# Three more warm-up matmuls of zeros in the prologue of an attention-plus-MLP kernel

## The chip, the core and the metric

The kernel runs on one core of one Trainium2 chip. The metric is the device time of one execution in microseconds (us); the median of several runs is compared. The profile is of one such execution and names the engines PE (TensorE's matmuls), PEld (TensorE's weight loads, which overlap the matmuls), DVE (VectorE), ACT (ScalarE), POOL (GpSimd) and SP (SyncE, which only issues transfers here).

## The reference

There are 8 batches and 8 heads, with 512 tokens and 32 state rows of 64 features in each. Tokens read the state and the state reads the tokens, both through a softmax; the results, 4352 rows of 512, then go through a two-layer MLP with SiLU.

```python
# x: (8, 8, 512, 64)   state: (8, 8, 32, 64)
a      = softmax(x @ state.T / 8)        # over the 32 state rows
xread  = a @ state
a2     = softmax(state @ x.T / 8)        # over the 512 tokens
sread  = a2 @ x
rows   = concat([xread, sread], axis=2)  # heads side by side: (4352, 512)
h      = rows @ w_in                     # (512, 2048)
g      = h * sigmoid(h)
out    = g @ w_out                       # (2048, 512), float32
```

## The kernel before

The schedule is written by hand: each engine executes its instructions in the order in which the program states them, and semaphores order the engines among one another. Matmuls take bf16 operands and sum in float32.

For each batch the first MLP layer is merged with the state: `w1_cols` (L336) multiplies the transposed state `stT` by `w_in` and evicts the product as `W1`. The attention weights are computed per group of four heads (`hg` 0 and 1): `scores` (L230), `exps` (L242, on ACT), `norm` (L252 to L255: sums and reciprocals on DVE, the product `an` on POOL or DVE) and a transpose into `aT`, which for batch 0 TensorE does itself (`pe_transpose_a`, L272). `emit_G1` (L362) multiplies W1 by aT and applies SiLU on ACT; `G2` (L391) multiplies the result by `w_out`, summing over 16 chunks of features, and `store` evicts and writes the rows. The state's own reads go through `token_sums`, `sread` (L293, L303) and a last pass at the end (L372, L413). From batch 0 on, the loops over `tt` and `ft` weave the next batch's attention in between the matmuls of the present one.

The change lies in the prologue. What it touches, in program order:

- SP issues the state of batch 0 (`st0_f`, the profile's `st_f`) and x of batch 0 in two halves of four heads (`x_f`, L139). POOL builds the identity and issues the first loads of `w_in`, `w_out` and the whole state (`st_b`).
- DVE clears `busy`, a tile of zeros, and `stT`.
- `keep_busy(n, pool, tag)` (L129) has TensorE multiply zeros by zeros n times, 128x128 by 128x512, into a PSUM tile of the given pool that nobody reads. Nothing waits for these matmuls except what is behind them in TensorE's own order, and later users of that PSUM buffer.
- The first `keep_busy` stands ahead of the transposes of batch 0's state (L163). DVE then copies these in four pieces into `stT` (L123).
- The second `keep_busy` follows, ahead of the transposes of x (L186), which wait for DVE's cast of x to bf16 (`cast_x`, L100, tile `x_nat`).
- After both groups' scores and exponentials, `w1_cols` for 256 columns and five loads issued by POOL, the third `keep_busy` stands ahead of the transposes of `an` (L272).

Of the kernel before, what the change touches and what calls it, by code (L numbers as in the profile page):

```python
# [36 lines left out]
def kernel(  # L37
# [20 lines left out]
    psO = ctx.enter_context(tc.tile_pool(name="psO", bufs=2, space=bass.MemoryType.PSUM))  # L58
    psH = ctx.enter_context(tc.tile_pool(name="psH", bufs=2, space=bass.MemoryType.PSUM))
# [34 lines left out]
    def load_x(b):  # L94
        nc.gpsimd.dma_start(x_f[:], x[b].rearrange("h (p c) d -> p h c d", p=128, c=4))  # L95
# [23 lines left out]
    def copy(eng, dst, src):  # L119
        if eng is nc.scalar:  # L120
            nc.scalar.activation(dst, src, func=COPY, bias=0.0)  # L121
        else:
            eng.tensor_copy(dst, src)  # L123


    def keep_busy(n, pool, tag):
        ps = pool.tile([128, 512], FP32, tag=tag, name="ps_busy")
        for _ in range(n):
            nc.tensor.matmul(  # L129
                ps[:], busy[:, 0:128], busy[:], start=True, stop=True, skip_group_check=True  # L130
            )
# [24 lines left out]
    )  # L156


    keep_busy(6, psH, "h1")
    copy(nc.vector, st0_n[:], st0_f[:])  # L160
    ps0 = bank([128, 4, NS], BF16, "ps_st0")
    for kt in range(4):
# [3 lines left out]
    for g in range(2):  # L166
        for u in range(2):
# [2 lines left out]
                stT[ds(64 * u, 64), 0, ds(2 * g, 2), u ^ g, :],  # L170
                ps0[ds(64 * u, 64), ds(2 * g, 2), :],
            )
    keep_busy(3, psH, "h1")

# [92 lines left out]
    def pe_transpose_a(b, hg, eng):  # L269
        ps = bank([128, 4, 128], BF16, "ps_at")  # L270
        for c in range(4):
            nc.tensor.transpose(ps[:, c, :], an[b, hg][:, c, :, :], ident[:])  # L272
        copy(eng, aT[b][:, hg, :, :], ps[:])
# [79 lines left out]
    h1 = {}  # L353
# [91 lines left out]
    load_w_in(1536)  # L445
    load_w_out(12, 4)
    load_x(1)
    keep_busy(3, psO, "o")
    pe_transpose_a(0, 0, nc.vector)
    pe_transpose_a(0, 1, nc.vector)  # L450

# [148 lines left out]
```

## Time and profile before

| | us |
|---|---|
| median of 5 runs | 225.04 |
| lowest and highest | 224.52 and 227.21 |
| the profiled execution's own time | 224.52 |
| its span, first to last instruction | 222.5 |
| PE busy | 211.4 (95%) |
| PEld busy | 100.8 (45%) |
| DVE busy | 104.9 (47%) |
| ACT busy | 142.4 (64%) |
| POOL busy | 45.7 (21%) |

A line of a timeline gives the start, the time from there to the end of the last of its instructions, the engine, the line of the kernel, what is written and read, and how many instructions are merged in it; in square brackets stands how long the engine had been idle before and what ended that. A line of the chain of waits has start, length and what it was; the chain runs backwards from the last instruction through whatever released each step. In the table by stretch, the columns are the stretch, its length, then busy time and count of PE, PEld, DVE, ACT and POOL, the granted TensorE clock as a share of full speed, the DMA share, and GB/s. The ends of matmuls are modelled: their starts are the surer record.

### The profile page before, as it was taken

The page shows a single profiled execution, that of the slowest core. Times are in us where ns is not written, and L with a number is a line of the kernel's source. Part 1 is how long each engine was busy: PE and PEld are TensorE (multiplying, and loading weights), DVE is VectorE, ACT ScalarE, POOL GpSimd, SP SyncE. Part 2 cuts the span into 40 slices and gives each one's busy share as a digit, 9 for nine tenths or more (in the row PEclk, how much of TensorE's full clock was granted, in tenths as well). Part 3 has the DMA queues.
Part 4 walks back from the last instruction along what each step waited for, and adds up shares of the span by engine and source line. Part 5 has one row for each costly group of instructions (what it writes and reads, how often), then busy time and mean ns, then how long its engine had stood idle before and what let it go on. Part 6 is the DMA issues. An engine that isn't in the chain of part 4 may idle for free.

```text
span 222.5 us, 3716 instructions
## 1 busy us (share of the span) xinstructions
PE 211.4 (95%) x1462; PEld 100.8 (45%) x1488; DVE 104.9 (47%) x183; ACT 142.4 (64%) x241; POOL 45.7 (21%) x64
## 2 busy tenths in 40 slices
PE   7689899999989999999999999999999999999993
PEld 2434235445425443545344444454454445466652
DVE  5665856452975075525644382629260836010011
ACT  2655469899555985588577947695759675834410
POOL 8480001800800045002700090008000300000000
PEclk9999999999999999999999999999999999999998
DMA  5999955393375115911594138504700330111112
GB/s 190 198 205 205 213 183 199 134 246 104 98 238 122 47 48 133 292 48 47 102 253 120 50 94 248 134 0 110 177 16 32 86 107 0 47 47 50 47 47 94
DMA packets 32209, 26.78 MB, mean 120 GB/s; under 512 B 20160, under 2 KB 26048, under 8 KB 32192
## 3 DMA queue, kind: packets, MB, share of 16 engines
q1 hardware_dynamic: 25376, 14.75, 24.2%
q0 software_dynamic: 6816, 11.80, 23.4%
q8 instruction: 11, 0.18, 0.3%
q14 instruction: 6, 0.05, 0.1%
HBM read 17.37 MB, written 8.91 MB: 118 GB/s over the span
## 4 chain that ended last, share of the span: by engine, by line
PE 84%; DVE 10%; issue 2%; ACT 1%; POOL 0%; DVEq 0%; POOLq 0%
PE o L391 44%; PE h L362 24%; PE ps_w L336 4%; PE h L372 3%; PE ps_sc L230 2%; DVE es_f L282 2%; DVE stT L123 2%; PE o_half L413 2%; DVE rb L312 2%; PE ps_sr L303 1%; DVE W L123 1%; PE ps_busy L129 1%; DVE xmT L316 1%; DVE rs L252 1%; ACT exp_nat L242 1%
## 5 line engine op out<-in xcount | busy, mean ns | idle before, releaser
L391 PE MATMUL o<-w_out_sb,g 128*128 128x512 bf16 x488 | 132.6, 379 | 1.0 <-issue 0.2
L383 ACT ACTIVATE g<-h 128x512 bf16<-128x512 f32 (+1 forms) x144 | 82.0, 573 | 41.5 <-PE h L362 27.2
L362 PE MATMUL h<-aT,W 128*128 128x512 bf16 x256 | 75.5, 379 | 2.3 <-DVE W L123 1.5
L391 PEld LDWEIGHTS <-g 128*128 128x128 bf16 x528 | 49.7, 98 | 58.1 <-issue 6.4
L123 DVE COPY o_sb<-o 128x512 f32<-128x512 f32 x17 | 11.8, 692 | 62.8 <-PE o L391 62.7
L362 PEld LDWEIGHTS <-W 128*128 128x128 bf16 x256 | 24.6, 98 | 32.3 <-DVE W L123 3.7
L255 POOL TENSOR_TENSOR an<-exp_nat,rc 128x512 bf16<-128x512 bf16 (+1 forms) x16 | 15.9, 1009 | 109.9 <-DVE rc L253 109.7
L123 DVE CAST W<-ps_w 128x512 bf16<-128x512 f32 (+1 forms) x31 | 20.0, 676 | 18.7 <-PE ps_w L336 18.7
L121 ACT ACTIVATE W<-ps_w 128x512 bf16<-128x512 f32 (+1 forms) x35 | 18.7, 575 | 11.4 <-PE ps_w L336 11.3
L312 DVE RECIPROCAL rb<-ps_sr 128x256 f32<-128x256 f32 x8 | 14.0, 1750 | 16.2 <-PE ps_sr L303 16.2
L121 ACT ACTIVATE o_sb<-o 128x512 f32<-128x512 f32 x15 | 8.9, 597 | 14.3 <-PE o L391 6.1
L282 DVE TENSOR_REDUCE es_f<-exp_nat 128x128 f32<-128x512 bf16 x16 | 15.5, 1013 | 0.2
L100 POOL CAST x_nat<-x_f 128x512 bf16<-128x512 f32 x24 | 14.7, 646 | 0.0
L336 PE MATMUL ps_w<-w_in_sb,stT 64*32 64x512 bf16 (+1 forms) x264 | 11.6, 376 | 0.6 <-DVE stT L123 0.4
L252 DVE TENSOR_REDUCE rs<-exp_nat 128x16 f32<-128x512 bf16 x16 | 10.6, 660 | 1.9 <-ACT exp_nat L242 1.2
L95 POOL DMA_DIRECT2D x_f<-in_x_dram x7 | 6.5, 926 | 19.8 <-DVE x_nat L100 18.3
L316 DVE TENSOR_TENSOR xmT<-ps_sr,rb 64x64 bf16<-64x64 f32 x32 | 9.6, 299 | 0.6
L372 PE MATMUL h<-xmT,w_in_sb 128*128 128x256 bf16 x64 | 9.6, 273 | 0.0
L242 ACT ACTIVATE exp_nat<-ps_sc 128x512 bf16<-128x512 f32 x16 | 8.8, 595 | 0.9 <-PE ps_sc L230 0.8
L372 PEld LDWEIGHTS <-w_in_sb 128*128 128x128 bf16 x64 | 6.3, 98 | 3.9
L242 ACT ACT_TABLE_LOAD x6 | 7.7, 1283 | 0.2 <-PE ps_sc L230 0.2
L537 ACT ACT_TABLE_LOAD x6 | 7.7, 1283 | 0.1
(56 smaller groups left out, 100.7 us busy)
## 6 DMA issues: line engine op xcount, KB each, us to landing
out_dram<-o_sb SPq DMA_DIRECT2D x33, 256.0 KB, 2.3
x_f<-in_x_dram POOLq DMA_DIRECT2D x7, 1024.0 KB, 7.1
w_in_sb<-in_moe_w_in_dram POOLq DMA_DIRECT2D x3, 512.0 KB, 10.1
w_out_sb<-in_moe_w_out_dram POOLq DMA_DIRECT2D x3, 512.0 KB, 12.0
x_f<-in_x_dram SPq DMA_DIRECT2D x2, 512.0 KB, 4.3
w_in_sb<-in_moe_w_in_dram POOLq DMA_DIRECT2D x2, 256.0 KB, 7.2
w_out_sb<-in_moe_w_out_dram POOLq DMA_DIRECT2D x2, 256.0 KB, 7.7
st_b<-in_state_dram POOLq DMA_DIRECT2D x1, 256.0 KB, 12.3
```

The source lines that it names most:

```text
L100: eng.tensor_copy(x_nat[b][:, ds(c0, nc_), ds(h0, nh), :], x_f[:, ds(h0, nh), ds(c0, nc_), :].rearrange("p h c d -> p c h d"),)
L121: nc.scalar.activation(dst, src, func=COPY, bias=0.0)
L123: eng.tensor_copy(dst, src)
L242: nc.scalar.activation(e[:], sc_ps[hg][:], func=EXP, bias=0.0, scale=SCALE)
L255: eng.tensor_tensor(a[:, ds(c, n)], e[:, ds(c, n)], rc[:, ds(c, n)].to_broadcast([128, n, 4, NS]), op=MULT,)
L282: nc.vector.tensor_reduce(f[:, hg], exp_nat[b, hg].rearrange("p c s n -> p s n c"), axis=AX, op=ADD)
L312: nc.vector.reciprocal(rb[:], ps[:, 1, :, :, :])
L336: nc.tensor.matmul(pss[f, hg][ds(32 * s, 32), 0:n], stT[ds(r, 64), b, h // 2, s % 2, :], w_in_sb[ds(r, 64), h // 2, ds(f, n)], start=True, ...
L362: nc.tensor.matmul(ps[:], W1[b][:, hg, ds(128 * ft, 128)], aT[b][:, hg, :, :], start=(hg == 0), stop=(hg == 1), skip_group_check=True,)
L372: nc.tensor.matmul(ps[:, 0:256], w_in_sb[:, kt, ds(128 * ft, 128)], xmT[:, :, kt].rearrange("p t n b -> p t (n b)"), start=(kt == 0), stop ...
L383: nc.scalar.activation(g[:, 0:n], ps[:, 0:n], func=SILU, bias=0.0)
L391: nc.tensor.matmul(outs[tt][:], gt[b * NFT + ft][:, ds(128 * tt, 128)], w_out_sb[:, ft, :], start=(ft == 0), stop=(ft == NFT - 1), skip_gr ...
```

## The change

Each of the three calls of `keep_busy` gets one more matmul of zeros: 6 becomes 7, and 3 becomes 4 twice. Everything else is as it was.

```diff
-    keep_busy(6, psH, "h1")
+    keep_busy(7, psH, "h1")
     copy(nc.vector, st0_n[:], st0_f[:])
     ps0 = bank([128, 4, NS], BF16, "ps_st0")
     for kt in range(4):
...
-    keep_busy(3, psH, "h1")
+    keep_busy(4, psH, "h1")
...
     load_w_out(12, 4)
     load_x(1)
-    keep_busy(3, psO, "o")
+    keep_busy(4, psO, "o")
     pe_transpose_a(0, 0, nc.vector)
     pe_transpose_a(0, 1, nc.vector)
```

## The prediction, made before the result was known

> **What bounds the kernel now.** I read the page first, then the chain of waits in order of time, then the timeline of the first 14 us, where the edit lies.
>
> ```profile
> span 222.5 us, 3716 instructions
> ...
> PE 211.4 (95%) x1462; PEld 100.8 (45%) x1488; DVE 104.9 (47%) x183; ACT 142.4 (64%) x241; POOL 45.7 (21%) x64
> ...
> PEclk9999999999999999999999999999999999999998
> ```
>
> TensorE is busy 95% of the span, and from 12.7 us on it runs almost without a hole. Ahead of that lies a prologue in which each engine waits for another. A delay there is not hidden: all that follows starts later by the same amount. So the question is whether the added matmuls lie on the prologue's path. The chain says that some of them do:
>
> ```profile
> 1.22 2.74 PE ps_busy L129 x6
> 3.96 0.23 PE ps_st L163 x4
> ...
> 5.01 0.03 issue
> 5.04 0.80 DVE x_nat L100
> 5.84 0.05 issue
> 5.89 0.78 PE ps_xt L186 x8
> ```
>
> The first six matmuls of zeros are a link of the chain. After them come the state transposes (L163), four DVE copies into stT, the cast of x, and the transposes of x. The timeline shows the same stretch by engine:
>
> ```profile
> 2.48 0.15 PEld L129 LDWEIGHTS <-busy 128*128 128x128 bf16 x1 [0.28 <-issue]
> 2.69 0.63 DVE L123 CAST st_n<-st_f 32x512 bf16<-32x512 f32 x1 [0.30 <-DMA st_f<-in_state_dram]
> 2.90 0.15 PEld L129 LDWEIGHTS <-busy 128*128 128x128 bf16 x1 [0.28 <-issue]
> ...
> 3.90 0.28 PE L163 MATMUL ps_st<-ident,st_n 32*128 32x32 bf16 x4
> ...
> 4.11 1.46 PE L129 MATMUL ps_busy<-busy 128*128 128x512 bf16 x3
> 4.21 0.80 DVE L123 COPY stT<-ps_st 64x64 bf16<-64x64 bf16 x4 [0.90 <-PE ps_st L163]
> ...
> 5.04 0.79 DVE L100 CAST x_nat<-x_f 128x1024 bf16<-128x1024 f32 x1
> ...
> 5.89 0.76 PE L186 MATMUL ps_xt<-ident,x_nat 128*128 128x128 bf16 x8 [0.32 <-DVE x_nat L100]
> ...
> 7.55 0.62 PE L186 MATMUL ps_xt<-ident,x_nat 128*128 128x128 bf16 x8
> ```
>
> The state's cast ended at 2.69 + 0.63 = 3.32, yet its transposes began at 3.90: they stood 0.58 us behind the zeros in TensorE's order. DVE then waited 0.90 us for them, and the cast of x follows the stT copies with no idle time of its own. Was x late? Its first half, in the DMA view of that issue alone:
>
> ```profile
> x_f<-in_x_dram SPq DMA_DIRECT2D x1, 512.0 KB, 3.7
> ```
>
> Issued at 1.21, it landed at about 1.21 + 3.7 = 4.91, and the cast began at 5.04. So x was there 0.13 us before DVE was free. The zeros already reach past the wait that they fill.
>
> **The change, part by part.**
>
> First place (6 to 7 matmuls, ahead of the state transposes). One more 512-column matmul. The weight loads of the zeros start 0.43 us apart (2.05, 2.48 and 2.90 in the timeline). The state transposes therefore start at 3.90 + 0.43 = 4.33, the stT copies end at 5.01 + 0.43 = 5.44, the cast of x runs from 5.47 to 6.26, and the transposes of x could start at 6.32 instead of 5.89. Nothing covers this: **+0.43 us** on the path.
>
> Here a rule and a row stand apart. The page's clock row and the table by stretch give 1.00 while the zeros run:
>
> ```profile
> 1.20:4.60 3.40, 3.38 (x12) 1.13 (x13) 2.05 (x6) 1.02 (x2) 3.27 (x6) 1.00 0.65 214
> ```
>
> By that row the added matmul costs what a 512-column one costs later: three of L362 take 0.81 us at 12.69 with the last one 0.38 long, (0.81 - 0.38) / 2 = 0.22. But the starts are 0.43 apart in this very stretch. The Trainium skill (TensorE: Matmul & The Clock Gate, Part 1) says that TensorE starts at half rate and gives 426.7 ns per 512-column matmul for that state, 215.7 ns for the full one. The spacing agrees with it, the clock row doesn't show it. By the row the sum would be +0.22, by spacing +0.43 here; I take the spacing.
>
> Second place (3 to 4, between state and x). Shifted, these zeros start at 4.11 + 0.43 = 4.54, and four at 0.43 leave TensorE free at 6.26, while x_nat lets it go on at 6.32. So the fourth is **hidden, +0.00**, by the 0.32 us that TensorE idled before L186. Its margin is only 0.06. Bounds: 0.00, and 0.04 if starting a transpose behind zeros costs as much as at 3.90, where it came a little late.
>
> What is late next: the clock. The first eight transposes of x took 0.76 us, the second eight 0.62: in the middle of the first set the spacing falls from 0.11 to 0.055 us, at about 6.2. If that edge stays where it is, the moved transposes (from 6.32) all run at the full rate and give back 0.76 - 0.62 = **-0.14**. A rule speaks against more than that. The same page and part says the warm-up is "~3.4 µs of time, not a number of matmuls", in windows that run free of the kernel. By it, zeros added where TensorE is already packed (3.38 busy of 3.40 us above) bring the edge no earlier. The trace has one edge, 5.0 us after the first matmul at 1.22, which allows it. By the rule the gain is 0.14; if the edge came forward by one matmul's 0.43, the four transposes that ran slowly are the most it could speed, and these are in the 0.14 already. So the end is the same.
>
> Third place (3 to 4, in the softmax). These run at the full rate:
>
> ```profile
> 9.31 0.82 PE L129 MATMUL ps_busy<-busy 128*128 128x512 bf16 x2
> ...
> 10.55 0.40 PE L272 MATMUL ps_at<-ident,an 128*128 128x128 bf16 x4 [0.41 <-POOL an L255]
> ```
>
> The last starts at 9.31 + 0.82 - 0.38 = 9.75 and the next could follow at 9.97; the added one makes this 10.19. L272 waits for POOL until 10.54: 0.35 us to spare, so **+0.00**. Even at the half rate four zeros would end at 9.31 + 1.72 = 11.03, and the path goes through the second `an`, whose transposes start at 11.78. All of this moves with the chain.
>
> Behind it. POOL's issues at 1.43 to 6.12 don't depend on TensorE and stay. Its later weight and x loads (11.67 to 14.67) follow its two `an` products and move by the same 0.29. Their landings either move too or, if bandwidth holds them, less; both keep the present margins: the 1024 columns of w_in land at 11.67 + 9.7 = 21.4 and are used at 22.45, x of batch 1 at 14.67 + 17.2 = 31.9 and is cast at 32.37. The second half of x landed at 1.69 + 4.9 = 6.6; its cast (6.81) moves to 7.1. From 12 to 60 us the listed waits of TensorE's matmuls are all for DVE or POOL, which move along, none for a landing; so I find nothing that swallows the delay later. No step adds a semaphore wait.
>
> Sum: +0.43 + 0.00 - 0.14 + 0.00 = **+0.29 us**. The profiled execution took 224.52 with a span of 222.5 (2.0 around it), so it would become 224.8, span 222.8. That execution is the fastest of the five; their median is 0.52 higher, and +0.29 on 225.04 gives **225.3**.
>
> **Rivals.**
>
> (a) The chain as above, +0.29; +0.47 if the edge isn't met (0.43 + 0.04); +0.08 if the added matmul costs only 0.22. So 225.1 to 225.5. I give it 0.66.
>
> (b) A steadier clock pays. The five runs spread from 224.52 to 227.21, and the fastest is the one whose trace has the edge at 6.2. If the windows run free, slower ones may have met their edge later, since TensorE idled from 5.57 to 5.89 and more after 6.65. The added zeros close that hole. An estimate: the median run gets rid of its 0.52 and pays 0.29, 224.8; with a further loss of other runs gone, 224.5. For: the spread. Against: one trace can't show other runs' edges, and the hole is only 0.3 us. To be faster by 1% it would have to go to 222.8, below the fastest run, which had its edge early. 0.24.
>
> (c) Slower by over 1%: the clock rises only at a later window. Place: the transposes and scores from 6.3 us and the dense matmuls from 12.7. An estimate with the page's 3.4 us windows: from 6.2 to 9.6 the two sets of transposes pay about 0.05 each on the path, sixteen in all, 0.8; two windows on, to 13.0, G1 adds 0.2 per matmul; three on, to 16.4, the 3.7 us of dense work since 12.7 lose half, 1.9. Sum 0.29 + 0.8 + 0.2 + 1.9 = 3.2, 228.2. To pass 2.25 us the edge must come after about 15 us (1.3 by 13 us, then half of each us). For: the run at 227.21 is of this size. Against: the edit adds activity ahead of the edge, it takes none away. 0.07.
>
> (d) The added zeros change nothing, because x was what was waited for: then +0.0, 225.0. The landing at 4.91 against DVE's 5.01 speaks against it. 0.03.
>
> **Numbers.** About 1%, 2.25 us, is what a measurement of this kernel can tell from no change. (a), (d) and nearly all of (b) lie within it, (c) beyond; a corner of (b), or a span that moved for another reason, is left to faster. That gives 0.03 faster, 0.90 same, 0.07 slower. The range reaches down to (b) with some of the runs' own scatter, 224.3, and up to the scatter above (a), 226.5.
>
> **What would show it.** In the changed trace: state transposes at 4.33, the cast of x at 5.47 with no idle time before it, L186 first at about 6.3 with eight in 0.62 us, idle before L186 nearly gone, L272 first at 10.8 with an idle of about 0.2 left, span 222.8. Wrong would be: L186 still at 5.9 (then x or another wait held it), L186 well after 6.35 (the second place isn't hidden), L362 spaced 0.43 at 13 us (case c), or a delay at 12.7 us that is gone by 60 us (something swallowed it).

## The result: faster by 0.4%, and the runs draw together

| | before | changed |
|---|---|---|
| runs | 80 | 43 |
| median, us | 225.81 | 224.94 |
| lowest, us | 224.25 | 224.38 |
| highest, us | 228.66 | 225.55 |

The ratio of changed to before is 0.9958, with a 95% interval of 0.9943 to 0.9974; it leaves out runs more than 1.5% above the fastest of their kernel. The median of 225.04 that the prediction started from was that of five runs; 80 runs give 225.81. The new median lies within the forecast range, but on the other side of before than +0.29. The best runs of the two kernels are alike. What is gone are the long ones: 43 of the 80 runs of before took more than 225.6 us, of the changed kernel none.

The profiled execution of the changed kernel took 225.05 us and has a span of 223.1, so it is *longer* than the one shown of before (224.52 and 222.5). One trace against one trace points the wrong way here, and it is worth seeing why. First the chain of waits of the changed kernel (start, length, what):

```profile
1.22 3.17 PE ps_busy L129 x7
4.39 0.22 PE ps_st L163 x4
...
5.43 0.03 issue
5.46 0.71 DVE x_nat L100
6.17 0.05 issue
6.21 0.64 PE ps_xt L186 x8
```

And its timeline of TensorE:

```profile
4.53 1.04 PE L129 MATMUL ps_busy<-busy 128*128 128x512 bf16 x4
...
6.21 0.62 PE L186 MATMUL ps_xt<-ident,x_nat 128*128 128x128 bf16 x8 [0.65 <-DVE x_nat L100]
...
10.73 0.40 PE L272 MATMUL ps_at<-ident,an 128*128 128x128 bf16 x4 [0.19 <-POOL an L255]
...
12.87 0.81 PE L362 MATMUL h<-aT,W 128*128 128x512 bf16 x3 [0.30 <-DVE aT L123]
```

The seventh zero moves the cast of x from 5.04 to 5.46, the transposes of x run at the full rate, and G1 arrives at 12.87 instead of 12.69: 0.18 later. A further 0.36 of the longer span is a wait at 52.8 us for a DMA transpose of batch 2's x, which a second trace of the same kernel (e10, span 222.7) doesn't have. So within this run the edit costs a little, as forecast, though not quite for the forecast reason: the four zeros of the second place start 0.22 apart, (1.04 - 0.38) / 3, so here the clock had risen by 4.5 us and not at 6.2, and TensorE then idled 0.65 us ahead of x. The gain lies in runs that the first trace of before didn't show.

In what follows, the granted TensorE clock of a run is its mean over the span, and runs are called long when they took more than 225.6 us.

### The profile page after: what moved, and what is told of

The parts are those of the page before. It is cut to its first block, busy times and chain, and to the rows that moved or that the text cites. A ratio compares the mean times of both kernels' runs of the same rounds, so it can differ in the third digit from the quotient of the medians.

```text
span 223.1 us, 3721 instructions
## 1 busy us (share of the span) xinstructions
PE 211.4 (95%) x1464; PEld 100.9 (45%) x1491; DVE 104.9 (47%) x183; ACT 142.4 (64%) x241; POOL 46.0 (21%) x64
## 3 DMA queue, kind: packets, MB, share of 16 engines
q0 software_dynamic: 6816, 11.80, 23.4%
## 4 chain that ended last, share of the span: by engine, by line
PE 78%; DVE 11%; DMA 4%; issue 2%; POOL 2%; ACT 2%; POOLq 0%; DVEq 0%
PE o L391 42%; PE h L362 21%; DMA xT<-x_nat 4%; PE ps_w L336 4%; PE h L372 3%; DVE es_f L282 2%; DVE stT L123 2%; PE ps_sc L230 2%; PE o_half L413 2%; DVE rb L312 2%; PE ps_sr L303 1%; PE ps_busy L129 1%; DVE W L123 1%; DVE rs L252 1%; ACT exp_nat L242 1%
## 5 line engine op out<-in xcount | busy, mean ns | idle before, releaser
L391 PE MATMUL o<-w_out_sb,g 128*128 128x512 bf16 x492 | 133.6, 379 | 1.0
L362 PE MATMUL h<-aT,W 128*128 128x512 bf16 x250 | 74.3, 379 | 2.2 <-DVE W L123 1.5
L391 PEld LDWEIGHTS <-g 128*128 128x128 bf16 x528 | 49.7, 98 | 58.1 <-issue 6.4
L362 PEld LDWEIGHTS <-W 128*128 128x128 bf16 x256 | 24.6, 98 | 32.3 <-DVE W L123 3.7
L121 ACT ACTIVATE W<-ps_w 128x512 bf16<-128x512 f32 (+1 forms) x35 | 18.7, 576 | 11.4 <-PE ps_w L336 11.3
```

The source lines that it names most:

```text
L362: nc.tensor.matmul(ps[:], W1[b][:, hg, ds(128 * ft, 128)], aT[b][:, hg, :, :], start=(hg == 0), stop=(hg == 1), skip_group_check=True,)
L391: nc.tensor.matmul(outs[tt][:], gt[b * NFT + ft][:, ds(128 * tt, 128)], w_out_sb[:, ft, :], start=(ft == 0), stop=(ft == NFT - 1), skip_gr ...
```

## The experiments

Three numbers stand for the places: (6, 3, 3) is before, (7, 4, 4) the change. For each kernel the runs are counted that show a granted clock of 0.992 or less ("fell"), and those above 225.6 us with a clock of 0.997 or more ("long, full"). The variants were measured in four series, each with runs of before beside it: e1 to e4 (75 runs of before, median 226.06), e5 to e8 (67, 226.26), e9 to e12 (37, 226.25) and e13 to e16 (27, 227.28). A ratio is always to the runs of before in the same series; medians of different series are not compared so closely, the last one least. The change's 60 runs are the 43 above, the profiled one and e10's 16.

| kernel | zeros | runs | median | lowest to highest | fell | long, full |
|---|---|---|---|---|---|---|
| before, all four series | 6, 3, 3 | 206 | 226.26 | 224.43 to 228.94 | 105 | 58 |
| the change, first runs and e10 | 7, 4, 4 | 60 | 224.94 and 224.77 | 224.38 to 225.55 | 0 | 0 |
| e1_first | 7, 3, 3 | 22 | 225.09 | 224.44 to 227.58 | 5 | 2 |
| e2_second | 6, 4, 3 | 22 | 225.09 | 224.04 to 227.30 | 7 | 1 |
| e3_third | 6, 3, 4 | 22 | 225.77 | 224.59 to 226.67 | 12 | 6 |
| e4_early | 5, 6, 4 | 22 | 224.90 | 224.27 to 225.68 | 1 | 1 |
| e5_first_second | 7, 4, 3 | 22 | 225.30 | 224.70 to 226.98 | 4 | 2 |
| e6_second_third | 6, 4, 4 | 22 | 225.68 | 224.54 to 226.89 | 11 | 2 |
| e7_555 | 5, 5, 5 | 22 | 225.28 | 224.77 to 226.87 | 5 | 0 |
| e8_hole | 6, 0, 4 | 14 | 226.56 | 225.77 to 227.25 | 1 | 13 |
| e9_no_zeros | 0, 0, 0 | 4 | 228.70 | 228.02 to 229.84 | 0 | 4 |
| e11_655 | 6, 5, 5 | 22 | 224.90 | 224.25 to 225.90 | 2 | 0 |
| e16_x_first | 6, 5, 5, x first | 22 | 227.13 | 226.48 to 228.74 | 4 | 18 |

### One place at a time (e1 to e3), and the same number of zeros put elsewhere (e4)

```diff
 e1: -    keep_busy(6, psH, "h1")
 e1: +    keep_busy(7, psH, "h1")
 e2: -    keep_busy(3, psH, "h1")
 e2: +    keep_busy(4, psH, "h1")
 e3: -    keep_busy(3, psO, "o")
 e3: +    keep_busy(4, psO, "o")
 e4: first place 6 -> 5, second 3 -> 6, third 3 -> 4
```

> Seven zeros in the first place, three in the second and third. Clock theory (the runs before differ by when TensorE's clock rises, and an unbroken stretch of matmuls up to x's transposes makes it rise early in every run): the hole ahead of L186 stays, some 0.3 to 0.5 us, so the runs still spread over 2 to 3 us, with a median of 225.5 to 226 and a lowest of 224.7. Length theory (only the number of zeros counts, wherever they stand): two thirds of the late runs are gone, median 225.1. Softmax theory (the third place does it): spread as before, median 226.1, 0.3 above before.

> Four zeros in the second place, the others as before. Clock theory: the hole of 0.3 us ahead of L186 is filled at no cost to the path, so most late runs go, median 224.7 to 225.0, lowest 224.3, spread near 1 us. Length theory: as with the first place alone, less its 0.43 us on the path, about 224.9. Softmax theory: as before, about 225.8 with a spread of 3 us.

> Four zeros in the third place, the others as before. Clock theory: it comes after 9.3 us and fills 0.2 us of a hole that is off the path; runs whose clock rose at 6 us gain nothing, later ones little: median within 0.3 of before, spread 3 us. Softmax theory: the late runs go, median 224.7 to 225.0, spread 1 us.

> Five zeros, then the state transposes, then six zeros, four in the third place: as many ahead of x's transposes as the change has, but the state transposes leave at 3.4 us instead of 4.3, so that the cast of x waits for x itself (landed about 4.9). Clock theory: TensorE is packed as long as in the change, so the late runs are gone too; x's transposes start at 5.8 where the clock has risen, at 6.2 where it has not: median 224.5, 0.4 below the change, spread 1 us. Path theory (zeros ahead of the state transposes cost 0.43 us each on the path and the clock does not matter): 224.5 as well, but with the spread of before, 3 us.

Against before's 226.06 in the same series the ratios are 0.9964 (0.9935 to 0.9994), 0.9968 (0.9941 to 0.9995), 0.9975 (0.9950 to 1.0000) and 0.9943 (0.9919 to 0.9967). The first or the second place alone removes many long runs, not all: 7 and 8 of 22 fell or were long with a full clock, of before in this series 53 of 75. e1's median is the 225.1 of the theory that only counts zeros, below the 225.5 to 226 of the clock theory, and e2's spread of 3.3 us is far above the 1 us expected. The third alone removes none by count, 18 of 22, but its worst run is 226.67 where before's is 227.85: among its 12 falls none shows 0.977 (15 of before's 34 do), the lowest of the three values. e4 has no more than one run above 225.6 and the median of the change, not the 0.4 less that was expected: its cast of x waited 0.77 us for x, which landed later than in before's first trace.

The traces of these runs brought what none of the theories held: the clock rises *and falls again*. In e2's profile (225.2 us span, clock 0.985), the table by stretch (stretch, length, busy time of PE, PEld, DVE, ACT and POOL, granted clock, DMA, GB/s) shows

```profile
9.00:10.00 1.00, 0.95 (x14) 0.32 (x11) 0.47 (x2) 0.84 (x2) 0.59 (x1) 1.00 1.44 201
10.00:11.00 1.00, 0.49 (x5) 0.23 (x4) 0.93 (x3) 1.00 (x1) 0.56 (x2) 1.00 1.25 205
11.00:12.00 1.00, 0.26 (x3) 0.27 (x4) 0.54 (x2) 0.79 (x4) 1.00 (x2) 0.70 1.25 206
12.00:13.00 1.00, 0.91 (x6) 0.39 (x4) 0.42 (x1) 0.00 (x0) 1.00 (x2) 0.50 1.24 208
...
17.00:18.00 1.00, 1.00 (x4) 0.34 (x3) 0.72 (x2) 0.52 (x1) 0.00 (x0) 0.50 1.11 196
18.00:20.00 2.00, 1.94 (x15) 0.56 (x14) 0.69 (x1) 1.08 (x2) 0.00 (x0) 0.94 1.25 210
```

The mean of 0.70 from 11 to 12 puts the fall at 11.4 (0.4 at 1.00 and 0.6 at 0.50); the 0.94 puts the return at 18.24. The dense matmuls of batch 0 run at half rate for most of what lies between. In e3's profile the same reading gives a fall at 8.82 and a return at 12.24; all that lies between is at half rate:

```profile
8.82:12.24 3.42, 3.11 (x23) 1.55 (x24) 2.24 (x6) 2.90 (x6) 1.81 (x3) 0.50 1.31 202
```

### Which holes (e5 to e8)

The theory was now that there are two holes: one ahead of x's transposes, where the rise is missed, and one in the softmax, where the clock falls.

```diff
 e5: first 6 -> 7, second 3 -> 4, third stays 3
 e6: first stays 6, second 3 -> 4, third 3 -> 4
 e7: first 6 -> 5, second 3 -> 5, third 3 -> 5
 e8: first stays 6, third 3 -> 4
-    keep_busy(3, psH, "h1")
```

> The change without its third place (7, 4, 3). Two-hole theory (the clock is judged at edges 3.4 us apart that run free of the kernel: in some runs it rises late, because zeros and x's transposes leave a hole, in others it falls again in the softmax, because too little runs there): no late rise, but about a quarter of the runs still fall in the softmax and show a granted clock of 0.992, 0.985 or 0.977 and 225.5 to 227.7 us; median 225.0 to 225.1, highest above 226.5. One-hole theory (only the stretch ahead of x's transposes matters): as the whole change, all runs between 224.4 and 225.6.

> The change without its first place (6, 4, 4). Two-hole theory: the falls in the softmax are gone and the second zero fills most of the hole ahead of x, so at most one run in ten rises late; no cost on the path: median 224.6, 0.3 below the whole change, highest perhaps 226. If the first place is needed: a fifth or more of the runs above 225.8 with a granted clock of 1.00.

> Five zeros in each place. The state transposes leave at 3.4 us, x's transposes at 5.8, and the softmax has two zeros more than before, within POOL's time for the first product. Two-hole theory: no falls, less than one run in ten rises late, median 224.5 to 224.6, 0.3 to 0.4 below the whole change. If the stretch ahead of x must reach 6.2 us as in the change: a fifth of the runs above 225.8, median 225.

> No zeros between the state's and x's transposes (6, 0, 4): TensorE idles from 4.1 to 5.9 us. Two-hole theory: in nearly all runs the clock rises only at a later edge, after 8 us, though the granted clock reads 0.99 to 1.00; median 226.0, lowest 225.3; in the trace the second set of x's transposes is still spaced 0.107 us. Path theory (nothing but the order of the work counts): 224.5 in the best runs, as before, since the path has no zeros less or more than before until 5.9 us.

e5 came out as expected in kind: without the third place 4 of 22 runs fall, in the change none of 60 (e5's two long runs with a full clock are at 225.67 and 225.69, just over the line). So the third zero, off the path, seems to help keep the clock up. That it is worth time is not shown: e5's median of 225.30 lies 0.2 above what was expected, but its ratio of 0.9946 (0.9924 to 0.9968) is no worse than the change's, which was not measured in this series. e8 came out in kind too: without the second place 13 of 14 runs are long with a full clock. Its median of 226.56 is 0.56 above the expected one. Its fastest run, 225.77, is the profiled one and of another kind: there the clock rose early and fell, so none of the 13 was seen in a trace.

e6 and e7 were misses. In e6, 11 of 22 runs fell although the softmax had its fourth zero; the expected median was 224.6, measured 225.68, and the ratio to before (226.26) is 0.9982, with 1.0006 as upper end. e7's median is 225.28, with 5 falls. So the first two places also matter for falls, not just for the rise. How, a trace of before itself showed.

### Before traced again, and no zeros at all (e9, e10, e12)

```diff
 e9: all three keep_busy calls deleted
 e10: the change as it is
 e12: before as it is
```

> No zeros at all (0, 0, 0). It shows what a late rise looks like in a trace. Two-hole theory: no window of 3.4 us is full before the dense matmuls, so every run rises late: G1's first matmuls at 12 us still start 0.43 us apart, while the granted clock reads 1.00 there; time 226.5 to 228, all runs in this band. Path theory (zeros in the first place hold the state transposes and with them x by 0.5 us, and the clock costs little): 224.5 or less.

> The change itself, on the same chip as the others of this call. Median 224.9 to 225.2, all runs within about 1.2 us, none with a granted clock of 0.992 or less. The path term of the prediction, +0.29, holds against the kernel before's undisturbed runs only if x lands at 4.9 in most runs; if it lands at 5.0 to 5.5, as in six of the ten traces so far, the lowest tenth of the kernel before is 0.1 or less below the lowest tenth of the change.

> The kernel before once more, for its trace. Two-hole theory: with a chance of a half it is one of the long runs (above 225.6), and then its trace shows either the clock falling between 7.5 and 13 us (granted clock 0.992 to 0.977 over the span) or x's second transposes still 0.107 us apart at 7.5 us. One-hole theory: only the latter. If it is a short run, the clock rose before 6.7 us and did not fall.

e12's run of before took 226.99 us with a clock of 0.977. Its timeline of TensorE:

```profile
4.08 0.82 PE L129 MATMUL ps_busy<-busy 128*128 128x512 bf16 x3
5.95 0.62 PE L186 MATMUL ps_xt<-ident,x_nat 128*128 128x128 bf16 x8 [1.04 <-DVE x_nat L100]
...
7.96 1.04 PE L186 MATMUL ps_xt<-ident,x_nat 128*128 128x128 bf16 x8 [0.31 <-DVE x_nat L100]
...
13.11 2.16 PE L362 MATMUL h<-aT,W 128*128 128x512 bf16 x4
```

and three rows of its table by stretch:

```profile
3.88:7.30 3.42, 1.98 (x21) 1.04 (x21) 2.14 (x7) 0.60 (x1) 2.86 (x5) 1.00 1.15 256
7.00:8.00 1.00, 0.59 (x9) 0.31 (x8) 0.69 (x1) 0.51 (x2) 0.00 (x0) 0.65 1.28 185
...
17.00:18.00 1.00, 1.00 (x5) 0.35 (x3) 0.97 (x2) 0.20 (x1) 0.00 (x0) 0.73 1.13 203
```

Here the clock was up before 4.1 us: three zeros take 0.82 us instead of 1.46. By that they end early, and TensorE idles 1.04 us ahead of x (0.32 in the trace that the prediction used). In the 3.42 us up to 7.3 TensorE is busy 1.98, and at 7.3 the clock falls, before the softmax; it returns at 17.5. So an early rise, lucky in itself, shortens the padding and opens the hole ahead of the fall. This is how the zeros ahead of x can count for falls too, and it would explain why e6, with one zero less there than the change, had so many; e6's own trace is of a run that did not fall, so for e6 it is not shown.

e9 shows the other kind. All its matmuls of 512 columns run at half rate up to 19 us, as in e13 below, while the clock row reads 1.00. Its ratio to before is 1.0112 (1.0049 to 1.0176), its median 228.70 above the band expected. e10 repeats the result, with a ratio of 0.9940 (0.9916 to 0.9963) and no falls in 16 runs; its median of 224.77 is 0.13 below the expected band.

### The same cover without moving the state (e11)

```diff
 e11: first stays 6, second 3 -> 5, third 3 -> 5
```

> Six, five and five zeros: TensorE is packed to the same moment as in the change (6.25 us at the half rate), but the state transposes are not moved, and the softmax has one zero more than the change. Two-hole theory: all runs in one band as with the change, median 224.8 to 224.9, 0.1 below it. If the first place must be seven: a tenth or more of the runs above 225.8, median at or above 225.2.

224.90 and a ratio of 0.9941 (0.9921 to 0.9962): as good as the change, not better, and two of 22 runs fell. The seventh zero in the first place is thus not needed as such. What the counts fit is that TensorE must stay occupied as far as x. Ordered by the zeros ahead of x, first and second place together, the runs that fell or were long with a full clock are:

| zeros ahead of x | kernels | fell or long, full |
|---|---|---|
| 0 and 6 | e9, e8 | 4 of 4, 14 of 14 |
| 9 | before, e3 | 163 of 206, 18 of 22 |
| 10 | e1, e2, e6, e7 | 7, 8, 13 and 5 of 22 |
| 11 | the change, e4, e5, e11 | 0 of 60, then 2, 6 and 2 of 22 |

The number of all zeros orders them less well: e7 has as many as the change and e4, 15. e16 below, which opens a hole of its own, is left out.

### Three more traces of before (e13 to e15), and x issued first (e16)

> The kernel before, for its trace once more. Two-hole theory: if the run is long (above 225.6) with a granted clock of 0.992 to 0.977, the clock fell at an edge 3.4 us or twice that after its rise; if it is long with 1.00, x's second transposes are 0.107 us apart and the clock rose after 7.5 us; if it is short, neither.

> The kernel before again. What is looked for is a long run (above 225.6) with a granted clock of 1.00, which the theory says rose late; about one run in four is of this kind.

> The kernel before again, for the same: a long run with a granted clock of 1.00 has x's second transposes 0.107 us apart; a long run with a lower granted clock has the fall in its trace.

e13 took 228.69 us and e14 228.87, both with a granted clock of 1.00; e15 took 226.14, with 0.985. The timeline of e13, first TensorE, then two rows of its table by stretch:

```profile
4.11 1.46 PE L129 MATMUL ps_busy<-busy 128*128 128x512 bf16 x3
6.62 1.03 PE L186 MATMUL ps_xt<-ident,x_nat 128*128 128x128 bf16 x8 [1.05 <-DVE x_nat L100]
...
13.71 2.16 PE L362 MATMUL h<-aT,W 128*128 128x512 bf16 x4
...
18.25 1.06 PE L391 MATMUL o<-w_out_sb,g 128*128 128x512 bf16 x2
...
20.48 0.61 PE L391 MATMUL o<-w_out_sb,g 128*128 128x512 bf16 x2
```

```profile
12.00:14.00 2.00, 1.53 (x10) 0.92 (x9) 1.18 (x5) 1.36 (x4) 1.54 (x2) 1.00 1.23 205
...
17.00:18.00 1.00, 1.00 (x4) 0.43 (x3) 1.00 (x2) 0.00 (x0) 0.14 (x1) 1.00 1.16 205
```

Four matmuls of L362 take 2.16 us (at 12.69 in before's first trace three took 0.81), with 1.00 in the clock's column all the while: a clock that has not yet risen is read as full. Only later, by 20.5 us, do two matmuls of L391 take 0.61 and no longer 1.06. These are the long runs with a full clock, seen in before itself; e14's trace is alike. What came late is in the DVE rows of e13:

```profile
4.21 0.80 DVE L123 COPY stT<-ps_st 64x64 bf16<-64x64 bf16 x4 [0.90 <-PE ps_st L163]
5.65 0.91 DVE L100 CAST x_nat<-x_f 128x1024 bf16<-128x1024 f32 x1 [0.65 <-DMA x_f<-in_x_dram]
```

x landed at 5.6, not at 4.9, so the hole ahead of x is 1.05 us. In the five traces of before the cast of x begins at 5.04, 5.01, 5.65, 5.59 and 5.84; in the last three, all of the series in which before was slowest, DVE waits for x. That such a hole makes the clock rise late is borne out by e8, whose program leaves out the zeros there. In a single run it also depends on where the edge falls: in e15 x came latest of the five, the hole was 1.06 us, and yet the clock had risen by 6.6 (eight transposes of x from there took 0.62). It fell at 9.26, after a stretch with TensorE busy 1.94 us:

```profile
5.84:9.26 3.42, 1.94 (x28) 1.41 (x28) 2.44 (x5) 1.59 (x3) 0.85 (x2) 1.00 1.31 203
```

So a fall needs no early rise: here the zeros had taken their full 1.46 us.

```diff
 (6, 5, 5), and:
-    nc.sync.dma_start(st0_f[:], state[0].rearrange("h n d -> n h d"))
     for hg in range(2):
         nc.sync.dma_start(
...
         )
+        if hg == 0:
+            nc.sync.dma_start(st0_f[:], state[0].rearrange("h n d -> n h d"))
```

> Six, five and five zeros, and SP issues the first half of x ahead of the state of batch 0, so that x lands about 0.5 us earlier. If x's landing (4.9 to 5.5 us) is what most runs wait for ahead of its cast, the cast follows the stT copies at 5.04 in every run and the median falls by 0.1 to 0.3 against six, five and five alone (224.9), to 224.6 to 224.8. If the zeros or DVE hold x's transposes, it stays at 224.9. If the state comes later than the six zeros (cast of the state after 3.9), it is longer by the difference.

e16 is no better than before: its ratio is 1.0029 (1.0005 to 1.0052), its median 227.13 beside before's 227.28. It is the last of the three cases: in its trace the state came so late behind x's first half that its cast began at 4.72 and its transposes at 5.19. TensorE idled from 3.9 to then, and 18 of 22 runs are long with a full clock. It doesn't answer what it was made for, how much is gained with x landed sooner and the state in time; that stays open.

## Why the prediction was wrong, point by point

**The steps of the path were right for the traced run, in part by luck.** Forecast and found in the changed trace: state transposes at 4.33 and 4.32, cast of x at 5.47 and 5.46 with no idle time, idle before L272 of about 0.2 and 0.19, eight transposes of x in 0.62, the fourth zeros of the second and third place off the path. L186 began at 6.21 and not 6.32, since the cast took 0.70 where before had 0.79. On the way to G1 that is +0.18 for a forecast of +0.29. The luck is in the clock. The idle time before L186 was to be nearly gone and is 0.65, because the clock had risen by 4.5 and the four zeros took 1.04 us. The -0.14, forecast from an edge at 6.2, came from that earlier edge. The margin of 0.06 in the second place, worked out at half rate, is therefore not seen in this trace; e6 bears it out, where four zeros from 4.12 did take 1.89 us and L186 still began at 5.88, as before's at 5.89.

**The step that failed is the one from this trace to the median.** The prediction put +0.29 on the median as if all runs were like the traced one, and the zeros' effect on the clock of other runs at nothing in its sum. The trace was that of the shortest of five runs; the clock had its edge at 6.2 and stayed up. Of 206 runs of before only 43 neither fell nor were long, with a mean of 224.89 (all below 225.6 by the way they are picked); the change has 224.91 over its 60 runs, all of them of this kind. So the change removes the long runs, and where the clock is well it shows neither a gain nor the +0.29: in e10's own series the means are 224.77 (6 runs of before) and 224.83 (16 of the change). Where the +0.29 went is not shown. x's scatter can hide part of it: in three of the five traces of before DVE waited for x until after 5.47, and there a cast moved to 5.47 costs nothing.

**Rival (b) was the right mechanism and mis-sized, 0.24 us where the median moved 0.87.** Two terms of it failed.

- "the hole is only 0.3 us": it is 1.04 in e12 and 1.05 in e13, through an early rise (short zeros) in one and a late x in the other.
- Only a late rise was priced, and no fall. By granted clock, the runs of before stand at 225.5 (22 runs near 0.992), 226.3 (43 near 0.985), 227.5 (40 at 0.977) and 226.85 (58 long with a full clock). Over all 206 runs they put the mean 1.4 us above 224.89, 0.85 of it through falls.

**The rule that I set against the change was read in one direction.** From fall to return e3 took 12.24 - 8.82 = 3.42, e2 18.24 - 11.40 = 6.84 and e12 17.54 - 7.30 = 10.24: one, two and three times 3.41 to 3.42. The Trainium skill (TensorE: Matmul & The Clock Gate, Part 1) has windows of about 3.4 us that run free of the kernel, and the traces agree as closely as their rows can tell. I drew from it that zeros can't bring an edge forward. But where the edges fall differs from run to run: before's clock rose at about 6.2 in its first trace, before 4.1 in e12 and after 19 in e13. The counts fit that the zeros decide in how many runs a window is full enough for the rise, or too empty to keep it. The table of states in the same part says that an idle window of about 3.4 us brings the half rate back. In the trace it need not be idle: TensorE was busy 2.05 of the 3.41 us up to e2's fall,

```profile
7.99:11.40 3.41, 2.05 (x25) 0.89 (x23) 2.78 (x7) 3.00 (x6) 1.55 (x2) 1.00 1.32 201
```

and the changed kernel kept its clock with 2.66 in the stretch that answers to it, its second window after the rise (in e10's trace with 2.18, from 8.38 to 11.80):

```profile
7.82:11.24 3.42, 2.66 (x31) 1.34 (x31) 2.44 (x6) 2.99 (x4) 1.17 (x2) 1.00 1.30 197
```

What measure of activity decides stays open: before's first trace kept its clock with 1.81 busy in the second window after its rise.

```profile
9.62:13.03 3.41, 1.81 (x13) 0.77 (x13) 2.12 (x5) 2.19 (x5) 2.97 (x4) 1.00 1.27 207
```

**That no wait behind the prologue is for a landing** held for e10 and failed by 0.36 us in the first changed trace, at 52.8.

**Rivals (c) and (d).** (c) priced a rise at 16.4 us at 3.2, of which 2.9 are the clock's. In e13 the rise came about one window later still, between 19 and 20.5, which by (c)'s own working (half of 3.4 us more) makes an estimate of 4.6. e13 and e14 paid some 3.8 to 4.0 (228.69 and 228.87, against 224.9), so the price was of the right size. But these are runs of before, and the change removes them. (d) fails in the changed trace, where the zeros do move the cast; in runs where x comes as late as in e13 to e15 the first place would cost nothing, as (d) has it.

## What to carry to other kernels

When a kernel's runs spread by more than an edit's worth, a profile of one run, the shortest above all, says little on what the edit does to the median: look first at how the runs differ. Price idle stretches of TensorE in a sparse prologue by the dense work behind them that may run at half rate, not by their own length; padding can then pay, here 0.4 to 0.6% for three matmuls. And read the clock from the spacing of equal matmuls in the first stretch, because the granted clock's row reads 1.00 until its first change.

## What was not expected of the hardware

- A granted clock of 1.00 over the span stood beside 228.69 us and matmuls 0.43 us apart up to 19 us (e13).
- A clock that rises sooner can be lost again: in e12 three zeros shrank from 1.46 to 0.82 us, the hole ahead of x grew to 1.04, and the half rate came back for 10.24 us.
- The landing of the first half of x, 512 KB issued at 1.21 us, came from 3.5 (e12) to 4.6 us (e15) later in runs of the same kernel.
